# Retention, softplus and squared-ReLU layers on one core: another order for the head and the first half tile

## The chip, the cores and the metric
The kernel runs on one core of one Trainium2 chip. The metric is the device time of one execution in microseconds. The engines named here are TensorE (PE; its weight loads are listed as PEld), VectorE (DVE), ScalarE (ACT) and SyncE (SP), which issues most of the DMAs.

## The reference, cut to what matters
```python
# q, k, v: 4 batches, 8 heads, 576 tokens, 64 per head
scores = q @ k.T / 8                       # per batch and head
ret = scores * gamma[h] ** (i - j)         # only where i >= j, else 0
x = (ret @ v), heads side by side          # 2304 tokens x 512
h = x @ w_in;  g = max(h, 0) + log1p(exp(-|h|));  x = g @ w_out      # 512 -> 2048 -> 512
h = x @ w_in2; r = max(h, 0); g = r * r;          x = g @ w_out2     # 512 -> 2048 -> 512
```

## The kernel before
Retention runs in chunks of two times 64 tokens: a chunk is 1 MB of q, k (one DMA) and k, v (another). Each half of a chunk has a place s, 0 or 1, on the lower or the upper 64 partitions. For a chunk the kernel computes scores (small 64x64 matmuls), multiplies them with a mask, adds k times v to a running state (`states`), copies the state for the next half (`next_state`, two ScalarE copies) and forms the outputs from the masked scores and from the carried state (`outputs`). `scaled` multiplies the outputs with decay factors; the factors are spread over the partitions by small matmuls (`spread`) and products (`make_xw`).

The dense layers keep precision by splitting each operand into a high part (rounded to fp32r) and a low part, so each product is three matmuls. A weight arrives packed and takes five operations: two on ScalarE (L151, L152), one on VectorE (L156, "word operation"), a cast on ScalarE (L184) and a difference on VectorE (L185, the remainder). This is a generator, `split_w`, that is advanced by `pump_step` or `pump_to`; three staging buffers hold raw weights, and `pump_load` issues the next load when a buffer is free.

The first layer walks over five tiles of tokens (512, 384, 512, 512, 384) in steps. A step j does `g1` (L505: 12 matmuls into one bank), softplus (three ScalarE operations in `softplus_a`, three VectorE operations in `softplus_b`), `split_g` (cast and low part of g) of step j-1, and `g2` (L557: 12 matmuls into four accumulators) of step j-2. Between them it does one or two "visits" of retention for later tokens (`attend`, `visit`), and takes weights further. The first tile is done in two halves: steps 0 to 7 take its first eight blocks of the hidden layer, then tile 1 runs, then the other eight blocks of tile 0; its input x is kept in HBM (`x0d`) meanwhile.

Ahead of the steps is the head: the first four chunks (512 tokens), written out by hand under `manual_schedule`, which keeps the order of the source. Keep-warm matmuls of a zero tile (`keep_warm`, two records each) fill the start. The head shares four PSUM banks with the accumulators, converts three weights, and computes g1 of steps 0 and 1 for the first 256 tokens (`EARLY_G1`). Steps 0 to 7 are ordered by the framework's planner, the steps after them by the source.

Of the kernel before, what the change touches and what calls it, by code (L numbers as in the profile page):

```python
# [7 lines left out]
F32 = mybir.dt.float32  # L8
# [4 lines left out]
ALU = mybir.AluOpType  # L13
# [32 lines left out]
def kernel(  # L46
# [53 lines left out]
    ps_acc = ctx.enter_context(tc.tile_pool(name="ps_acc", bufs=4, space=PSUM))  # L100
# [3 lines left out]
    dram = ctx.enter_context(tc.tile_pool(name="dram", bufs=1, space=DRAM))  # L104

# [200 lines left out]

    x_raw = {}
# [126 lines left out]
    def scaled(c, s, po):  # L434
        m, _ = turn(c, s)
        t, off = tile_of((2 * c + s) * CN)
        if t == 0:
            x = ew.tile([P, 512], F32, tag="l", name="x")[:, :KD * CN]
            x = x.rearrange("p (a b) -> p a b", a=KD)
        else:  # L440
            if t not in x_raw:
                x_raw[t] = xs.tile([P, 512 // CN, KD, CN], F32, tag="xr", name="xr")
            x = x_raw[t][:, off // CN]
        xw = cst[:, C_XW + m * 256:C_XW + (m + 1) * 256].rearrange("p (a b) -> p a b", a=KD)
        nc.vector.tensor_tensor(out=x, in0=po, in1=xw, op=ALU.mult)
        if t == 0:
            h, l = (o[:, :, off:off + CN] for o in (x_hi(), x_lo()))
            nc.scalar.copy(h, x)
            return lambda: nc.vector.tensor_tensor(out=l, in0=x, in1=h, op=ALU.subtract)
# [37 lines left out]
    def in_heads(t):  # L487
        return t.rearrange("p (h c) -> p h c", c=CN)

    def g1(key, f, n, begin=0):
        if begin == 0:
            hps[key] = h_bank("ph")
        ph = hps[key]
        wh, wl = w_hi[0, "wi", f], w_lo[0, "wi", f]
        todo, rest = [], []
        for kk in range(KD):
            c = slice(kk * P, (kk + 1) * P)
            h, l = x_hi()[:, kk, begin:n], x_lo()[:, kk, begin:n]  # L500
            todo += [(wh[:, c], h), (wl[:, c], h)]
            rest.append((wh[:, c], l))
        todo += rest
        for j, (a, x) in enumerate(todo):
            nc.tensor.matmul(  # L505
                ph[:, begin:n], lhsT=a, rhs=x, start=(begin == j == 0),
                stop=(j == len(todo) - 1), skip_group_check=True,
            )
# [438 lines left out]
    EARLY_G1 = 2  # L947
    last = n_first
    with tc.manual_schedule():
        rows_in = xs.tile([P, SCN * KD * CN], F32, tag="xr", name="rows_in")  # L950
        for row in (0, CN):
# [3 lines left out]
        for half in (LO, HI):  # L955
            nc.scalar.dma_start(out=cst[half, :C_XW], in_=consts[CN:P, :C_XW])
# [24 lines left out]

        def acc_bank(name):
            return in_heads(ps_acc.tile([P, 512], F32, tag="at", name=name))[:, :HH]


        def early_s(c):
            pb = in_heads(ps_acc.tile([P, 512], F32, tag="at", name="pb"))
            for h in range(H):
                for half in (LO, HI):
                    nc.tensor.matmul(  # L990
                        pb[half, h, :], lhsT=chunk[c][half, 1, h, :], rhs=chunk[c][half, 0, h, :],
                        start=True, stop=True, skip_group_check=True,
                    )
            scale_v(c)
            nc.vector.tensor_tensor(
                out=chunk[c][:, 1], in0=pb,
                in1=cst[:, C_MASK:C_MASK + CN].unsqueeze(1).to_broadcast([P, H, CN]), op=ALU.mult,
            )

        pos = {}  # L1000

        def early_o(c):
            pos[c] = po = [acc_bank("po") for _ in range(2)]
            rounds(at_rounds((0, states(c, 0))), {})
            next_state(c, 0)
            rounds(
                at_rounds((0, outputs(c, 0, po[0]))),
                at_rounds((5, outputs(c, 1, po[1], False)), (13, states(c, 1))),
            )

        def early_x(c):
            for rest in [scaled(c, s, pos[c][s]) for s in range(2)]:
                rest()
            next_state(c, 1)

        early_s(0)
        early_o(0)
        early_x(0)
        early_s(1)
        make_xw(4, 5)  # L1020
        early_o(1)
        pump_step()
        early_x(1)
        pump_step()
        early_s(2)
        pump_step()
        early_o(2)
        early_s(3)
        early_x(2)
        g1(0, 0, P * 2)  # L1030
        pump_step()
        early_o(3)
        pump_step()
        g1(1, 1, P * 2)
        early_x(3)
        pump_step()
    tc.no_sync_barrier()
    for c in range(last):
        chunk.pop(c)
    first.__exit__(None, None, None)  # L1040
    late_wts.append(ctx.enter_context(tc.tile_pool(name="late", bufs=1, reuse_waits="tile")))
    tick[0] = 2 * last
# [3 lines left out]
    def visit(c, s):  # L1046
# [71 lines left out]
    def step(j, at_s, i):  # L1118
# [4 lines left out]
        g1(j, f, n, 2 * P if j < EARLY_G1 else 0)  # L1123
# [6 lines left out]
        for fn in low[:2]:  # L1130
            fn()
        softplus_b(j, n)
        for fn in low[2:]:
            fn()
        if j >= 1:
            split_g(j - 1, TILES[steps[j - 1][0]][1])
# [3 lines left out]
        if begun or n_split[0] < n_one:  # L1140
            pump_to(j)
        if done:
            done()
        if at_s == 0 and 0 <= i - (FH - 1 - KD) < KD:
            keep_x(i - (FH - 1 - KD))
# [22 lines left out]

    begun = []

    def pump_to(j):
        for made in begun:
            while not next(made):
                pass
            pump_load(n_used[0] + STAGES)
        begun.clear()
        goal = min(n_one, 4 + 2 * j if j < FH else 3 + 2 * FH + (j - FH))
        while n_split[0] < goal:
            count, make, args = items[n_split[0]]
            pump_load(n_used[0] + count)  # L1180
            made = make(*args)
            next(made)
            next(made)
            n_split[0] += 1
            n_used[0] += count
            begun.append(made)
# [7 lines left out]
    run(0, FH)  # L1194
    with tc.manual_schedule():
        run(FH, KF*last_b)
    run(KF*last_b, len(steps))
# [80 lines left out]
```

## Time and profile before
| what | value |
|---|---|
| median of 3 runs | 859.21 us (857.04 to 859.52) |
| profiled execution | 860.09 us, its span 858.3 us |
| busy share of the span | PE 98%, PEld 90%, DVE 79%, ACT 55% |
| clock granted to TensorE, mean | 0.981 |
| HBM read, written | 147.41 MB, 40.89 MB |

A granted clock of 1.00 is 2.4 GHz, 0.50 is 1.2 GHz. The shares are averages over stages with different limits, so they say little of the first 115 us, which the change touches. A busy PE is not a PE at its peak: records overlap, and their number and length both count.

### The profile page before, as it was taken

What the parts mean: (1) busy time and instruction counts of PE and PEld (TensorE: products, weight loads), DVE (VectorE), ACT (ScalarE), POOL (GpSimd) and SP (SyncE); (2) the same over time, 40 slices, a digit from 0 to 9 for tenths busy, and PEclk for the clock granted to TensorE, in tenths of its full rate; (3) what the DMA queues carried; (4) which work ended last, traced back from release to release, by engine and by line L of the source; (5) the groups of instructions that cost most, each with busy time, mean ns of one, the idle gap of its engine ahead of it and who ended that gap; (6) DMA issues with size and microseconds to landing.
All of it is one profiled execution on the core that took longest, in us unless ns stands there. A gap on an engine that the chain in (4) does not pass through costs nothing.

```text
span 858.3 us, 17849 instructions
## 1 busy us (share of the span) xinstructions
PE 839.0 (98%) x6688; PEld 768.6 (90%) x6688; DVE 680.6 (79%) x1266; ACT 473.9 (55%) x888; POOL 0.2 (0%) x4
## 2 busy tenths in 40 slices
PE   8899999999999999999999999999999999999998
PEld 7877799988788886888899999999999999999998
DVE  4579988878878878787899988888597986686964
ACT  4568888757656676676878621355321454111453
POOL 0000000000000000000000000000000000000000
PEclk9769999999999999999999999999999999999999
DMA  9337645545556664576676877888988888888885
GB/s 344 123 128 233 206 155 172 174 159 176 155 204 207 208 200 150 180 227 202 185 247 214 263 227 248 260 274 282 294 257 251 246 261 265 282 251 254 244 263 163
DMA packets 119512, 189.47 MB, mean 221 GB/s; under 512 B 10242, under 2 KB 64130, under 8 KB 119426
## 3 DMA queue, kind: packets, MB, share of 16 engines
q1 hardware_dynamic: 119264, 188.26, 68.9%
q8 instruction: 53, 0.87, 0.4%
q14 instruction: 31, 0.25, 0.1%
q10 hardware_dynamic: 164, 0.09, 0.0%
HBM read 147.41 MB, written 40.89 MB: 219 GB/s over the span
## 4 chain that ended last, share of the span: by engine, by line
PE 78%; DVE 9%; DMA 6%; ACT 5%; issue 2%; SPq 0%; DVEq 0%; ACTq 0%
PE acc L557 17%; PE ph L505 16%; PE py L758 9%; PE py L693 9%; PE pz L758 6%; PE px L693 6%; PE pz L693 6%; PE px L758 5%; PE po L417 2%; DVE l L529 1%; DVE e L526 1%; DMA wo_raw<-in_moe_w_out_dram 1%; PE st L394 1%; DMA ring<-in_qk_t_dram 1%; PE pb L369 1%
## 5 line engine op out<-in xcount | busy, mean ns | idle before, releaser
L505 PE MATMUL ph<-xh,wi 128*128 128x512 f32 (+2 forms) x656 | 149.0, 368 | 2.1 <-DVE ring L379 1.9
L505 PEld LDWEIGHTS ph<-xh,wi 128*128 128x128 f32 x656 | 119.6, 191 | 19.7 <-ACT ring L405 1.6
L557 PE MATMUL acc<-gl,woh 128*128 128x512 f32 (+1 forms) x320 | 120.1, 375 | 1.6 <-DVE gl L542 1.6
L557 PE MATMUL acc<-gh,woh 128*128 128x512 f32 (+1 forms) x320 | 121.0, 383 | 0.0
L557 PE MATMUL acc<-gh,wol 128*128 128x512 f32 (+1 forms) x320 | 119.4, 373 | 0.2 <-DVE wol L185 0.2
L526 DVE SCALAR_TENSOR_TENSOR e<-e 128x512 f32<-128x512 f32 (+1 forms) x80 | 51.0, 637 | 47.5 <-ACT l L521 46.5
L693 PE MATMUL py<-t,sring 128*128 128x384 f32 x432 | 88.2, 338 | 0.0
L505 PE MATMUL ph<-xl,wi 128*128 128x512 f32 (+2 forms) x328 | 81.8, 367 | 3.8 <-DVE xl L469 3.5
L519 ACT ACTIVATE e<-ph 128x512 f32<-128x512 f32 (+1 forms) x80 | 44.2, 553 | 65.9 <-PE ph L505 65.5
L693 PEld LDWEIGHTS py<-t,sring 128*128 128x128 f32 x432 | 75.3, 188 | 1.9 <-DVE uring L871 0.6
L505 PEld LDWEIGHTS ph<-xl,wi 128*128 128x128 f32 x328 | 59.9, 190 | 13.5 <-DVE xl L469 6.4
L557 PEld LDWEIGHTS acc<-gl,woh 128*128 128x128 f32 x320 | 60.7, 190 | 10.8 <-DVE gl L542 3.4
L557 PEld LDWEIGHTS acc<-gh,woh 128*128 128x128 f32 x320 | 60.8, 191 | 9.2 <-ACT gh L541 0.5
L733 ACT CAST gh<-g 128x384 fp32r<-128x384 f32 x84 | 43.0, 513 | 46.8 <-PE px L758 16.7
L557 PEld LDWEIGHTS acc<-gh,wol 128*128 128x128 f32 x320 | 60.8, 190 | 8.3 <-DVE wol L185 0.6
L733 ACT CAST gring<-g 128x384 fp32r<-128x384 f32 x84 | 43.2, 514 | 42.7 <-PE py L758 18.7
L719 DVE TENSOR_TENSOR gl<-g,gh 128x384 fp32r<-128x384 f32 x84 | 46.3, 556 | 19.2 <-ACT gh L733 18.9
L719 DVE TENSOR_TENSOR gring<-g,gring 128x384 fp32r<-128x384 f32 x84 | 46.7, 555 | 18.4 <-ACT gring L733 16.4
L867 ACT COPY uring<-px 128x384 f32<-128x384 f32 x24 | 11.5, 479 | 86.9 <-PE px L693 86.9
L693 PE MATMUL pz<-t,sring 128*128 128x384 f32 x288 | 58.7, 334 | 0.0
L693 PE MATMUL px<-t,sring 128*128 128x384 f32 x288 | 58.3, 336 | 0.0
L521 ACT ACTIVATE l<-e,cst 128x512 f32<-128x512 f32 (+1 forms) x80 | 54.5, 681 | 5.2 <-DMA x2d<-xo 1.8
(112 smaller groups left out, 1675.5 us busy)
## 6 DMA issues: line engine op xcount, KB each, us to landing
sring<-s2d SPq DMA_DIRECT2D x168, 256.0 KB, 3.2
sring<-o2d SPq DMA_DIRECT2D x168, 256.0 KB, 3.4
wi_raw<-in_moe_w_in_dram SPq DMA_DIRECT2D x32, 512.0 KB, 4.3
wo_raw<-in_moe_w_out_dram SPq DMA_DIRECT2D x32, 512.0 KB, 4.1
s2d<-ct SPq DMA_DIRECT2D x48, 256.0 KB, 2.6
o2d<-ct SPq DMA_DIRECT2D x48, 256.0 KB, 2.9
ring<-in_qk_t_dram SPq DMA_DIRECT2D x14, 512.0 KB, 4.9
ring<-in_kv_dram SPq DMA_DIRECT2D x14, 512.0 KB, 5.8
```

Source lines behind the costliest of these rows:

```text
L369: nc.tensor.matmul(pb[to, h, :], lhsT=kk[:, hh, :], rhs=qp[:, hh, :], start=True, stop=True, skip_group_check=True,)
L417: nc.tensor.matmul(po[(LO, HI)[hh % 2], hh // 2, :], lhsT=before[rows, hh, :] if carried else sv[:, hh, :], rhs=qp[:, hh, :] if carried el ...
L505: nc.tensor.matmul(ph[:, begin:n], lhsT=a, rhs=x, start=(begin == j == 0), stop=(j == len(todo) - 1), skip_group_check=True,)
L519: nc.scalar.activation(out=e, in_=ph[:, :n], func=AF.Abs)
L521: nc.scalar.activation(out=l, in_=e, func=AF.Ln, bias=below_one, scale=1.0 + 2.0**-23)
L526: nc.vector.scalar_tensor_tensor(out=e, in0=e, scalar=-2.0, in1=e, op0=ALU.add, op1=ALU.mult)
L557: nc.tensor.matmul(acc[j][:, :n], lhsT=a, rhs=x, start=(begin and m == 0), stop=(end and m == 2))
L693: nc.tensor.matmul(ps, lhsT=a, rhs=x, start=(first and m == 0), stop=(m == len(todo) - 1), skip_group_check=True,)
L719: nc.vector.tensor_tensor(out=out, in0=a, in1=b, op=ALU.subtract)
L733: nc.scalar.copy(h, src)
L758: nc.tensor.matmul(blocks[m], lhsT=a, rhs=x, start=(first and p == n == 0 and m in opens), stop=(p == NP - 1 and n == 2), skip_group_check ...
L867: nc.scalar.copy(s1, px)
```

## The change
The head gets its own four PSUM banks (`ps_head`, given back before the accumulators are made). It loads all four chunks before any weight. It handles both halves of a chunk in one VectorE operation of 512 elements where it used two of 256 (`early_x`, `early_low`), and interleaves the outputs of chunk c with the scores of chunk c+1, one half beside the other. It converts one weight in full and begins two more; the early halves of g1 go. The inputs x of the first tile are stored to `x0d` from the head by ScalarE's DMA queue; the four sums in `keep_x` go. Steps 0 to 7 run in source order, g1 of step 0 multiplies the high weights first, weights begun in a step are finished right after the next step's g1, and chunk 5 is loaded in step 0.
```diff
+    head = tc.tile_pool(name="ps_head", bufs=1, space=PSUM)
...
+    def pump_end():
+        for made in begun:
+            while not next(made):
+                pass
+            pump_load(n_used[0] + STAGES)
+        begun.clear()
...
-    def g1(key, f, n, begin=0):
+    def g1(key, f, n):
...
+        if key:
+            todo = [[w for two in zip(*todo[:2]) for w in two], todo[2]]
+        else:
+            todo = [todo[0], todo[2], todo[1]]
...
-    def keep_x(kk):
-        t = cvt.tile([P, 512], F32, tag="ct", name="x0")
-        nc.vector.tensor_tensor(
-            out=t, in0=x_hi()[:, kk].bitcast(F32), in1=x_lo()[:, kk].bitcast(F32), op=ALU.add
-        )
-        nc.sync.dma_start(out=x0d[:, kk], in_=t)
...
     def spread(dst, row, shape, eng):
-        rows = ps_acc.tile([P, 512], F32, tag="at", name="rows")[:, :shape[0] * shape[1]]
+        rows = ps_head.tile([P, 512], F32, tag="pb1", name="rows")[:, :shape[0] * shape[1]]
...
-        pump_load(1)
-        load_chunk(0)
-        load_chunk(1)
-        pump_load(2)
-        load_chunk(2)
-        load_chunk(3)
+        for c in range(last):
+            load_chunk(c)
         pump_load(3)
         load_chunk(last)
-        load_chunk(last + 1)
...
-        keep_warm(10)
+        keep_warm(18)
...
-        make_xw(1, 3)
-        keep_warm(10)
-        pump(1)
+        make_xw(1, 1)
+        keep_warm(3)
...
+        def early_o(c):
+            pos[c] = ps_head.tile([P, 2, 512], F32, tag="po", name="po")
+            po = [in_heads(pos[c][:, s])[:, :HH] for s in range(2)]
+            lower, upper = outputs(c, 0, po[0]), outputs(c, 1, po[1], False) + states(c, 1)
+            if c + 1 < last:
+                lower += early_scores(c + 1, LO)
+                upper += early_scores(c + 1, HI)
+            rounds(at_rounds((0, lower)), at_rounds((1, upper)))
+            next_state(c, 1)
+
+        def early_x(c):
...
+            nc.vector.tensor_tensor(
+                out=x, in0=pos.pop(c)[:, :, :256].rearrange("p s (a b) -> p s a b", a=KD),
+                in1=table[:, m:m + 2], op=ALU.mult,
             )
+            nc.scalar.copy(early_at(x_hi(), c), x)
+            kept_of.append(kept)
+
+        def early_keep(c):
+            nc.scalar.dma_start(out=x0d[:, :, c * P:(c + 1) * P], in_=kept_of[c])
...
+        rounds(at_rounds((0, early_scores(0, LO))), at_rounds((0, early_scores(0, HI))))
+        scale_v(0)
+        early_mask(0)
+        keep_warm(4)
+        make_xw(2, 2)
+        early_states(0)
         early_o(0)
+        scale_v(1)
         early_x(0)
+        early_mask(1)
+        early_states(1)
+        early_low(0)
         make_xw(4, 5)
...
+        early_mask(3)
+        early_states(3)
+        early_low(2)
         pump_step()
         early_o(3)
+        keep_warm(8)
+        early_x(3)
+        early_keep(2)
         pump_step()
-        g1(1, 1, P * 2)
-        early_x(3)
+        early_low(3)
         pump_step()
+        pump_begin(3)
+        early_keep(3)
...
-            pb = in_heads(h_bank("pb", False))[:, :HH]
+            if c == last:
+                pb = in_heads(ps_at.tile([P, 512], F32, tag="at", name="pb"))[:, :HH]
+            else:
+                pb = in_heads(h_bank("pb", False))[:, :HH]
...
-        g1(j, f, n, 2 * P if j < EARLY_G1 else 0)
+        g1(j, f, n)
+        if at_s == 0 and i < FH - 1:
+            pump_end()
...
-        if begun or n_split[0] < n_one:
-            pump_to(j)
+        pump_end()
+        pump_to(j)
+        if j == 0:
+            load_chunk(last + 1)
...
-    run(0, FH)
+    run(0, 0)
     with tc.manual_schedule():
-        run(FH, KF*last_b)
+        run(0, KF * last_b)
```

## Rows read from the trace of the kernel before
**Rows 1.** Busy time by stage: stretch, length, busy us, granted clock, DMA share, GB/s.
```profile
8.00:20.40 12.40, 9.73 (x245) 9.22 (x245) 8.37 (x15) 5.77 (x13) 0.00 (x0) 0.99 1.03 393
20.40:33.50 13.10, 12.62 (x202) 12.00 (x200) 6.40 (x13) 5.18 (x13) 0.00 (x0) 0.50 0.43 160
...
44.50:57.60 13.10, 13.10 (x129) 9.76 (x126) 10.07 (x21) 7.59 (x14) 0.00 (x0) 0.50 0.17 58
...
70.00:95.70 25.70, 23.85 (x279) 18.71 (x278) 23.75 (x44) 22.90 (x42) 0.00 (x0) 1.00 0.77 253
95.70:113.80 18.10, 17.76 (x123) 15.62 (x121) 15.10 (x28) 14.60 (x27) 0.00 (x0) 1.00 0.58 184
113.80:160.00 46.20, 46.16 (x387) 45.40 (x388) 39.78 (x74) 40.62 (x77) 0.00 (x0) 1.00 0.45 142
```
**Rows 2.** Timeline of PE, gaps before the clock fell: start, length, work, idle before.
```profile
19.07 0.27 PE L417 MATMUL po<-ch,ring 64*64 64x64 f32 x2 [1.31 <-issue]
...
44.20 0.79 PE L394 MATMUL st<-ring 64*64 64x64 f32 x9 [3.17 <-ACT ring L405]
```
**Rows 3.** Timeline of PE in the head.
```profile
1.04 4.64 PE L912 MATMUL cold<-warm 128*128 128x128 f32 x20 [1.04 <-DVE warm L906]
5.61 1.28 PE L929 MATMUL rows<-rows_in,ones 1*64 1x256 f32 x8
6.82 4.00 PE L912 MATMUL cold<-warm 128*128 128x128 f32 x20
10.75 1.15 PE L990 MATMUL pb<-ch 64*64 64x64 f32 x32
...
25.38 1.23 PE L417 MATMUL po<-ch 64*64 64x64 f32 x32
...
34.27 0.69 PE L417 MATMUL po<-ch 64*64 64x64 f32 x32
34.80 0.63 PE L417 MATMUL po<-ch,ring 64*64 64x64 f32 x16
```
**Rows 4.** Timeline of PE, steps 7, 8 and 11.
```profile
90.48 2.08 PE L505 MATMUL ph<-xh,wi 128*128 128x512 f32 x8 [1.21 <-DVE ring L379]
...
93.30 0.39 PE L557 MATMUL acc<-gh,woh 128*128 128x512 f32 x1
...
96.02 1.57 PE L505 MATMUL ph<-xh,wi 128*128 128x384 f32 x8
...
112.11 0.86 PE L505 MATMUL ph<-xl,wi 128*128 128x384 f32 x4
```
**Rows 5.** Timeline of ACT, softplus of step 7 and weight operations.
```profile
95.70 0.60 ACT L519 ACTIVATE e<-ph 128x512 f32<-128x512 f32 x1
...
97.00 0.73 ACT L521 ACTIVATE l<-e,cst 128x512 f32<-128x512 f32 x1
...
101.19 0.62 ACT L184 CAST wi<-ct 128x512 fp32r<-128x512 f32 x1
...
102.23 0.67 ACT L151 ACTIVATE wi_raw<-wi_raw 128x512 f32<-128x512 f32 x1
102.80 0.75 ACT L152 ACTIVATE wi_raw<-wi_raw,cst 128x512 uint32<-128x512 uint16 x1
```
**Rows 6.** Timeline of DVE, steps 3 and 7 and the drain.
```profile
64.49 0.68 DVE L532 SCALAR_TENSOR_TENSOR e<-ph,l 128x512 f32<-128x512 f32 x1
65.09 0.41 DVE L445 TENSOR_TENSOR xr<-po,cst 128x256 f32<-128x256 f32 x1
...
96.13 1.96 DVE L469 TENSOR_TENSOR xl<-xr,xh 128x384 fp32r<-128x384 f32 x4
...
108.56 1.28 DVE L567 COPY xo<-acc 128x512 f32<-128x512 f32 x2
```
**Rows 7.** DMA issues up to 110 us: KB each, median us from issue to landing.
```profile
wi_raw<-in_moe_w_in_dram SPq DMA_DIRECT2D x12, 512.0 KB, 4.2
...
ring<-in_qk_t_dram SPq DMA_DIRECT2D x5, 512.0 KB, 7.2
```

More of the change, by code (lines that the diff above doesn't have):

```diff
@@ L104 @@
     dram = ctx.enter_context(tc.tile_pool(name="dram", bufs=1, space=DRAM))
+    head = tc.tile_pool(name="ps_head", bufs=1, space=PSUM)
+    ps_head = head.__enter__()
     cst = const.tile([P, C_ALL], F32, name="cst")
@@ L304, in pump, with pump_begin @@
                     break
+    begun = []
+    def pump_end():
[4 more added lines that the diff above has]
+        begun.clear()
+    def pump_begin(upto):
+        while n_split[0] < min(n_one, upto):
+            count, make, args = items[n_split[0]]
+            pump_load(n_used[0] + count)
+            made = make(*args)
+            next(made)
+            next(made)
+            n_split[0] += 1
+            n_used[0] += count
+            begun.append(made)
     x_raw = {}
@@ L436, in scaled @@
         t, off = tile_of((2 * c + s) * CN)
[L437 to L443, printed above, removed]
-        xw = cst[:, C_XW + m * 256:C_XW + (m + 1) * 256].rearrange("p (a b) -> p a b", a=KD)
[L445 to L449, printed above, removed]
+        if t not in x_raw:
+            x_raw[t] = xs.tile([P, 512 // CN, KD, CN], F32, tag="xr", name="xr")
+        xw = cst[:, C_XW + m * 256:C_XW + (m + 1) * 256].rearrange("p (a b) -> p a b", a=KD)
+        nc.vector.tensor_tensor(out=x_raw[t][:, off // CN], in0=po, in1=xw, op=ALU.mult)
     tick = [0]
@@ L488, in in_heads @@
         return t.rearrange("p (h c) -> p h c", c=CN)
-    def g1(key, f, n, begin=0):
-        if begin == 0:
-            hps[key] = h_bank("ph")
-        ph = hps[key]
+    def g1(key, f, n):
+        ph = hps[key] = h_bank("ph")
         wh, wl = w_hi[0, "wi", f], w_lo[0, "wi", f]
-        todo, rest = [], []
+        todo = [[], [], []]
         for kk in range(KD):
             c = slice(kk * P, (kk + 1) * P)
[L500 to L503, printed above, removed]
+            h, l = x_hi()[:, kk, :n], x_lo()[:, kk, :n]
+            for part, a, x in zip(todo, (wh, wl, wh), (h, h, l)):
+                part.append((a[:, c], x))
+        if key:
+            todo = [[w for two in zip(*todo[:2]) for w in two], todo[2]]
+        else:
+            todo = [todo[0], todo[2], todo[1]]
+        todo = sum(todo, [])
         for j, (a, x) in enumerate(todo):
             nc.tensor.matmul(
-                ph[:, begin:n], lhsT=a, rhs=x, start=(begin == j == 0),
-                stop=(j == len(todo) - 1), skip_group_check=True,
+                ph[:, :n], lhsT=a, rhs=x, start=(j == 0), stop=(j == len(todo) - 1)
             )
@@ L945, in make_xw @@
         )
-    EARLY_G1 = 2
     last = n_first
@@ L950 @@
         rows_in = xs.tile([P, SCN * KD * CN], F32, tag="xr", name="rows_in")
+        for half in (LO, HI):
+            nc.scalar.dma_start(out=cst[half, :C_XW], in_=consts[CN:P, :C_XW])
         for row in (0, CN):
@@ L977 @@
         spread(times, row[:, 1:, :, 0], (SCN - 1, KD), nc.scalar.copy)
-        make_xw(1, 3)
-        keep_warm(10)
-        pump(1)
[L982 to L994, printed above, removed]
+        make_xw(1, 1)
@@ new lines, with early_scores @@
+        keep_warm(3)
+        pbs, pos, xs_of, kept_of = {}, {}, {}, []
+        def early_scores(c, half):
+            if c not in pbs:
+                pbs[c] = in_heads(ps_head.tile([P, 512], F32, tag=f"pb{c % 2}", name="pb"))
+            return [
+                lambda h=h: nc.tensor.matmul(
+                    pbs[c][half, h, :], lhsT=chunk[c][half, 1, h, :], rhs=chunk[c][half, 0, h, :],
+                    start=True, stop=True, skip_group_check=True,
+                ) for h in range(H)
+            ]
@@ L995, in early_s, with early_mask, early_states @@
+        def early_mask(c):
             nc.vector.tensor_tensor(
-                out=chunk[c][:, 1], in0=pb,
+                out=chunk[c][:, 1], in0=pbs.pop(c),
                 in1=cst[:, C_MASK:C_MASK + CN].unsqueeze(1).to_broadcast([P, H, CN]), op=ALU.mult,
             )
-        pos = {}
-        def early_o(c):
-            pos[c] = po = [acc_bank("po") for _ in range(2)]
+        def early_states(c):
             rounds(at_rounds((0, states(c, 0))), {})
             next_state(c, 0)
-            rounds(
-                at_rounds((0, outputs(c, 0, po[0]))),
-                at_rounds((5, outputs(c, 1, po[1], False)), (13, states(c, 1))),
-            )
@@ L1011, in early_x @@
[L1011 to L1016, printed above, removed]
+        def early_o(c):
[7 more added lines that the diff above has]
+            next_state(c, 1)
@@ new lines, in early_x @@
+        def early_x(c):
+            m = 2 * c
+            x = ew.tile([P, 512], F32, tag="e", name="x", bufs=3)
+            kept = x.rearrange("p (a n) -> p a n", a=KD)
+            x = xs_of[c] = x.rearrange("p (a s b) -> p s a b", s=2, a=KD)
+            table = cst[:, C_XW:].rearrange("p (m a b) -> p m a b", a=KD, b=CN)
+            nc.vector.tensor_tensor(
+                out=x, in0=pos.pop(c)[:, :, :256].rearrange("p s (a b) -> p s a b", a=KD),
+                in1=table[:, m:m + 2], op=ALU.mult,
+            )
+            nc.scalar.copy(early_at(x_hi(), c), x)
+            kept_of.append(kept)
@@ new lines, in early_keep, with early_at, early_low @@
+        def early_keep(c):
+            nc.scalar.dma_start(out=x0d[:, :, c * P:(c + 1) * P], in_=kept_of[c])
+        def early_at(t, c):
+            return t[:, :, c * P:(c + 1) * P].rearrange("p a (s b) -> p s a b", s=2)
+        def early_low(c):
+            nc.vector.tensor_tensor(
+                out=early_at(x_lo(), c), in0=xs_of.pop(c), in1=early_at(x_hi(), c),
+                op=ALU.subtract,
+            )
+        rounds(at_rounds((0, early_scores(0, LO))), at_rounds((0, early_scores(0, HI))))
@@ L1017 @@
+        scale_v(0)
[3 more added lines that the diff above has]
+        early_states(0)
         early_o(0)
+        scale_v(1)
         early_x(0)
-        early_s(1)
+        early_mask(1)
+        early_states(1)
+        early_low(0)
         make_xw(4, 5)
         early_o(1)
-        pump_step()
+        scale_v(2)
         early_x(1)
-        pump_step()
-        early_s(2)
-        pump_step()
+        early_keep(0)
+        early_mask(2)
+        early_states(2)
@@ L1039 @@
         chunk.pop(c)
+    head.__exit__(None, None, None)
     first.__exit__(None, None, None)
     late_wts.append(ctx.enter_context(tc.tile_pool(name="late", bufs=1, reuse_waits="tile")))
+    ps_acc = ctx.enter_context(tc.tile_pool(name="ps_acc", bufs=4, space=PSUM))
     tick[0] = 2 * last
@@ L1129, in step @@
         later = attend(at_s, i)
-        for fn in low[:2]:
+        if False and j:
+            split_g(j - 1, TILES[steps[j - 1][0]][1])
+        for fn in low:
             fn()
         softplus_b(j, n)
-        for fn in low[2:]:
-            fn()
-        if j >= 1:
+        if j and not (False):
             split_g(j - 1, TILES[steps[j - 1][0]][1])
@@ L1166, in step @@
                     build_t(m)
-    begun = []
     def pump_to(j):
[L1172 to L1186, printed above, removed]
+        pump_begin(4 + 2*j if j<FH else 3+2*FH+(j-FH))
     order = [(at_s, i) for at_s, (_, f0, f1) in enumerate(segments) for i in range(f1 - f0)]
@@ L1192, in run @@
             step(j, *order[j])
-    run(0, FH)
+    run(0, 0)
     with tc.manual_schedule():
-        run(FH, KF*last_b)
-    run(KF*last_b, len(steps))
+        run(0, KF * last_b)
+    run(KF * last_b, len(steps))
     j = len(steps)
```

10 lines of the change are left out of this document (3 added, 7 removed).

## The prediction, on record before the changed kernel was run
> **What bounds the kernel now.** I read the busy time by stage first, then the timelines of TensorE, ScalarE and VectorE over the first 115 us, and last the DMA issues. In the stages the reader sees two stretches of about 13 us each in which the granted clock is 0.50, the lower level of 1.2 GHz: 20.4 to 33.5 (the head, all small 64x64 matmuls) and 44.5 to 57.6 (steps 0 to 2) [rows 1]. Before the first fall TensorE ran small matmuls with gaps, the longest 1.31 us; before the second it sat idle for 3.17 us, waiting for ScalarE's state copies [rows 2]. From 70 to 95.7 VectorE is busy 23.75 of 25.70 us and TensorE 23.85. From 95.7 on TensorE is last: 17.76 of 18.10, then 46.16 of 46.20 [rows 1]. So I read the change at one mark, the end of g1 of step 11, 112.11 + 0.86 = 112.97 [rows 4]. Behind it the program is the same and TensorE sets the pace: what is gained or lost by then is gained or lost in the whole.
>
> I call S(j) the start of step j's first softplus operation on ScalarE (before: S(7) = 95.70 [rows 5]).
>
> **The change, part by part.**
> *Start.* Ten keep-warm pairs end at 1.04 + 4.64, ten more cost 4.00 [rows 3], so 0.40 each; eighteen end at 8.9. The spread took 1.28 with two banks; now both rows share one bank, so the second waits for the copy of the first. That wait is not in the trace. From below it is 0; from above a whole second spread, 1.28. I take 0.7, since only one copy lies between: 10.9. Three pairs: 12.1, and there the scores of chunk 0 begin, 1.35 later than the 10.75 of before [rows 3]. They take 1.15 (1.0 to the next start), four pairs 1.6 cover the mask: 14.75.
>
> *Chunks.* Matmuls of one half alone go 16 in 0.63, of both halves in two banks 32 in 0.69 [rows 3]; less the tail of about 0.15 that all share that is 33 and 17 ns. The new order runs outputs, states and next scores of the two halves beside each other. The longer, upper half sets it: 32 + 16 + 16 records at 33 ns, 2.1, with its lag and the same-bank rounds 2.4. Before each goes states(c,0), 0.55, and a wait for the state copies of about 0.3; the mask (0.7) runs beside these. About 3.35 a chunk. Chunk 0 goes 14.75 to 17.75, chunk 1 to 21.1, chunk 2 to 24.5, chunk 3, without next scores, to 27.2, where its outputs ended at 34.80 + 0.63 = 35.4 before [rows 3]. VectorE needs four operations of 0.60 to 0.69 a chunk, so 2.6, beside it. The wider operation on two banks is not in the trace; bounds are 0.60, a plain 128x512 operation, and twice that; I take the first, the same element count [rows 6]. The second bound would add under 1 us in all, since it waits beside the scores.
>
> *First matmul step.* Eight pairs, 3.2, end at 30.4. Beside them VectorE scales (27.6), ScalarE copies the state and casts x (28.6) and casts the first weight (about 29.6). Then g1(0) at the full clock, 93.30 - 90.48 = 2.8 [rows 4]: 33.2. The early halves of g1 in the head go; they were the same matmuls, so nothing is lost there. ScalarE has two weights begun (four operations, 2.5 [rows 5]), two DMA issues of 0.4 and two casts: S(0) at 33.5.
>
> *Step 0.* It holds two visits of chunk 4 that share a bank: scores, mask (behind the two weight remainders on VectorE), scale of v, then states and scores, then mask again, and only then softplus' VectorE part. With VectorE's starts 0.60 apart (65.09 - 64.49 [rows 6]) that part ends at 39.8, the weight's word operation at 40.4, its cast on ScalarE at 41.0; with full durations instead it is 42.4. I take S(1) = 42.0. TensorE idles nearly 3 us between the two visits, as it did before the second fall; if the clock falls there, g1(1) costs up to 2.8 more, of which softplus of step 1 sees about 0.5, as it waits for ScalarE anyhow.
>
> *Steps 1 to 6.* Source order closes a loop between two engines: softplus on ScalarE (95.70 to 97.73, 2.0 [rows 5]), three VectorE operations of 0.68, each waiting for the one before (2.0), the low part of g 0.60, scaled outputs 0.41, scale of v 0.60 in every second step, two word operations 1.2 [rows 6], a cast of 0.52 [rows 5], some 0.3 of handing over: 7.0 or 7.6. ScalarE alone needs 6.6, VectorE 6.3, TensorE 2.8 for g1, 96.02 - 93.30 = 2.7 for g2 [rows 4] and about 1.15 for a visit (32 small matmuls [rows 3]), 6.7 together, so the loop is last. S(6) = 42.0 + 7.6 + 7.0 + 7.6 + 7.0 + 7.6 = 78.8. The four sums of x (0.60 each) are gone from this stretch; their stores are the four ScalarE issues in the head, 1.6, half of it beside TensorE.
>
> *Loads.* Chunks first: 4.3 MB at 393 GB/s [rows 1] land by 13, three weights by 17, chunk 4 by 20, all before use (15 for chunk 1, 24 and 33 for the others). Chunk 5 is now issued at about 33 behind three weights; a chunk's q and k took 7.2 us from issue to landing [rows 7], so 40, and its visit is due at about 40: up to 1 us of TensorE, beside S(1). The second weight of each step is issued when its buffer comes free, about 1.2 before S(j), and wanted 4.4 after it; 4.2 to landing [rows 7] leaves about 1.
>
> *Into tile 1.* From S(6): casts of the new x on VectorE at 6.9, its four low parts 1.96 [rows 6], 8.8; softplus 2.0 and the low part of g, 11.4; g2(6) 2.7, g1(9) 2.1 (8 of its 12 take 1.57 [rows 4]): 16.2; g2(7), waiting for its low part until 16.4, 19.1; g1(10) 21.2; the four banks are drained (the VectorE pair 1.28 [rows 6]) by 23.2, g2(8) ends at 24.1, g1(11) at 26.2.
>
> *Sum.* The mark comes at 78.8 + 26.2 = 105.0 instead of 112.97: 8.0 gained. The profiled execution took 860.09 (span 858.3 and 1.8 around it), so 852.1; it lies 0.9 above the median of the runs, so against the median I forecast **851.5**.
>
> **The clock in the head** is the widest open point. What rows show: it fell at 20.4, some 9.6 us after the last full-array matmul, in a stretch that was busy 9.73 of 12.40 us, and then small matmuls at 12.62 of 13.10 did not raise it [rows 1]; full-array g1 did. After the change the small matmuls run from 14.75 to 27.2, 12.5 us, with fuller overlap and gaps under 0.8 us. The Trainium skill ("TensorE: Matmul & The Clock Gate", section "Why this matters for your kernels") ties throughput drops to idle gaps between bursts of matmuls and asks for continuous work. By that rule the head stays at 2.4 GHz and the sum holds; the trace agrees at the second fall (3.17 us idle), less at the first (1.31 us at most). If instead small matmuls alone let it fall, and as long after the last full-array one as before, it falls at 14.75 + 9.6, about 24.
>
> **Rivals.**
> *A, the head goes to 1.2 GHz at 20 to 22.* For it: 32 matmuls took 1.23 at the lower level against 0.69 [rows 3], and small matmuls alone held neither level before. Against it: gaps are shorter than where it fell. Price: chunks 2 and 3 cost some 5.3 more, and the eight pairs about 1.7 more; g1(0) comes at 37.5, S(1) is 5.5 to 6 later. Gain 2 to 2.5, 857.
> *B, in-order waits (slower).* With source order ScalarE's queue stops at the first operation on a weight that has not landed, and softplus of the next step is behind it; before, the order let other work pass. The mechanism sits at the second weight of each step and decides from a landing more than 5.6 us after issue. If weights take the 7.2 of the chunks they share the engines with [rows 7], each of steps 1 to 6 costs 1.6 to 2 more, 10 in all: gain -2, 861 to 862, and more where a chunk load goes ahead of them. Against it: the weights' 4.2, and DMA busy only 0.77 from 70 to 95.7 [rows 1].
> *C, the loop is shorter than I hold,* TensorE's 6.7 sets the step and S(1) is 41: S(6) at 74.5, gain 12, 847.
> *D, the new order isn't a new order:* the engines' order came out much as before and only the chunk part differs; then steps 1 to 7 keep their length and 1 to 2 us remain, 858.
>
> **How the numbers follow.** Forecast 0.58 (848.5 to 855), A 0.19, B 0.11, C 0.08, D 0.04. A change under 0.3% (2.6 us) can't be told from none here, so "same" is 856.6 to 861.8. Faster: forecast and C whole and half of A, 0.75; same: half of A, D and a little of B, 0.15; slower: most of B, 0.10. The range is 846.5 to 859, which leaves out B and the tail of C.
>
> **What would show it.** Right: granted clock 1.00 up to 30 us; last chunk's outputs at about 27, g1(0) at about 30; S(0) to S(7) 7 to 7.6 apart with VectorE's word operations as releaser of ScalarE's casts; g1(11) ending near 105. Wrong: a clock of 0.50 before 25 (A); ScalarE idle with weight DMAs as releaser in steps 1 to 6 (B); TensorE without gaps from step 1 (C). The forecast fails if the mark is later than 110.

## The result, and the profile after

| | median | executions |
|---|---|---|
| before | 859.28 us | 857.04 to 863.58 (6) |
| after | 848.75 us | 847.87 to 851.23 (6) |

Ratio 0.988, 95% interval 0.9852 to 0.9908: faster by 10.5 us, forecast 7.7. The profiled execution after took 847.87, its span 846.1 (before 858.3), its mean granted clock 0.996 (before 0.981).

Busy time by stage after, the columns and stretches of [rows 1]:

```profile
8.00:20.40 12.40, 10.36 (x272) 8.89 (x272) 7.45 (x11) 3.29 (x9) 0.00 (x0) 0.95 1.03 379
20.40:33.50 13.10, 12.80 (x285) 11.52 (x281) 7.99 (x13) 10.06 (x21) 0.00 (x0) 0.91 0.45 123
44.50:57.60 13.10, 12.06 (x153) 9.47 (x153) 11.99 (x22) 11.87 (x21) 0.00 (x0) 1.00 0.63 204
70.00:95.70 25.70, 22.22 (x183) 18.30 (x184) 23.12 (x42) 23.75 (x44) 0.00 (x0) 1.00 0.61 203
95.70:113.80 18.10, 17.76 (x153) 16.34 (x152) 14.75 (x28) 14.96 (x30) 0.00 (x0) 1.00 0.55 173
113.80:160.00 46.20, 46.20 (x365) 45.49 (x364) 38.26 (x71) 40.02 (x75) 0.00 (x0) 1.00 0.53 160
```

Where [rows 1] show 0.99, 0.50 and 0.50 the reader sees 0.95, 0.91 and 1.00. TensorE after, the lines that answer to [rows 2 to 4]:

```profile
1.04 6.45 PE L918 MATMUL cold<-warm 128*128 128x128 f32 x36 [1.04 <-DVE warm L912]
...
10.75 1.15 PE L988 MATMUL pb<-ch 64*64 64x64 f32 x32
...
18.45 0.27 PE L439 MATMUL po<-ch,ring 64*64 64x64 f32 x2 [1.43 <-issue]
...
28.13 2.05 PE L918 MATMUL cold<-warm 128*128 128x128 f32 x16
30.47 1.19 PE L519 MATMUL ph<-xh,wi 128*128 128x512 f32 x4 [0.29 <-ACT wi L185]
...
35.99 0.86 PE L391 MATMUL pb<-ring 64*64 64x64 f32 x16 [1.89 <-DVE ring L401]
...
105.30 0.86 PE L519 MATMUL ph<-xl,wi 128*128 128x384 f32 x4
```

The scores of chunk 0 start at 10.75, as before. The chunks are over at 28.13, some 7 us earlier than before, g1(0) (g1 of step 0) starts at 30.47, and the mark, the end of g1(11), is 105.30 + 0.86 = 106.16, so 6.8 us earlier [rows 4]. The gap of 1.43 at 18.45 is one that the forecast did not hold; the clock was at 0.50 behind it, from 19.27 to 22.68, and again behind the gap at 35.99, from 36.34 to 39.75.

ScalarE after, three of the starts S(j) and a cast that waits, the view of [rows 5]:

```profile
63.75 0.60 ACT L532 ACTIVATE e<-ph 128x512 f32<-128x512 f32 x1
...
71.06 0.60 ACT L532 ACTIVATE e<-ph 128x512 f32<-128x512 f32 x1
...
78.00 0.62 ACT L185 CAST wi<-ct 128x512 fp32r<-128x512 f32 x1 [1.31 <-DVE ct L157]
...
79.25 0.60 ACT L532 ACTIVATE e<-ph 128x512 f32<-128x512 f32 x1
```

The casts wait for VectorE's word operation ("<-DVE ct L157"): the loop between the two engines that the forecast drew. Steps 1 to 5 took 7.6, 7.3, 7.6, 7.3 and 8.2.

How far a kernel is ahead of the kernel before at S(j), from such lines of five profiled executions, one of each kernel. "Low alone", "without low" and "planner" are experiments below:

| | before | after | after is ahead by | low alone | without low | planner |
|---|---|---|---|---|---|---|
| S(0) | 39.49 | 34.27 | 5.2 | 0.9 | 4.3 | 4.0 |
| S(7) | 95.70 | 85.94 | 9.8 | 2.1 | 7.0 | 8.3 |
| S(9), tile 1 | 103.49 | 96.86 | 6.6 | 1.7 | 0.3 | 8.4 |
| S(31) | 216.71 | 210.15 | 6.6 | 1.7 | 0.3 | 8.3 |
| S(32), tile 2 | 224.42 | 215.82 | 8.6 | 3.7 | 0.3 | 10.4 |
| S(48), tile 3 | 328.56 | 319.16 | 9.4 | 4.8 | 0.3 | 11.4 |
| S(79), end of tile 4 | 490.01 | 477.44 | 12.6 | 7.3 | 0.3 | 13.9 |

The lead of 6.6 at S(9) stays to S(31) and then grows by 6.0, at the starts of tiles 2, 3 and 4 and within tile 4. The head can't do that. One line of the change does, `for fn in low[:2]` made `for fn in low`: where a new tile begins all four low parts of the next tile's x now go ahead of the VectorE part of softplus, where two went ahead and two behind. The cut diff ahead of the prediction leaves it out. What it does at the start of tile 2, before; first VectorE, then TensorE, then the stages:

```profile
219.29 1.29 DVE L469 TENSOR_TENSOR xl<-xr,xh 128x512 fp32r<-128x512 f32 x2
...
222.55 1.28 DVE L469 TENSOR_TENSOR xl<-xr,xh 128x512 fp32r<-128x512 f32 x2
```

```profile
223.28 1.10 PE L505 MATMUL ph<-xl,wi 128*128 128x512 f32 x2 [1.77 <-DVE xl L469]
...
325.13 1.10 PE L505 MATMUL ph<-xl,wi 128*128 128x512 f32 x2 [1.68 <-DVE xl L469]
```

```profile
224.00:228.00 4.00, 4.00 (x71) 3.16 (x72) 3.76 (x7) 3.51 (x7) 0.00 (x0) 0.63 0.45 145
```

The second pair of low parts starts 3.3 us after the first, and TensorE stands 1.77 us for it; then the clock is 0.63 in the mean of 224 to 228. At the start of tile 3 the same wait is 1.68 (second line of TensorE), and there the clock stays at 1.00. After, at the start of tile 2, in the same views (the stage 8 us earlier, as this kernel is 8.6 ahead there):

```profile
212.73 2.49 DVE L482 TENSOR_TENSOR xl<-xr,xh 128x512 fp32r<-128x512 f32 x4
215.14 0.69 DVE L539 SCALAR_TENSOR_TENSOR e<-e 128x512 f32<-128x512 f32 x1
```

```profile
214.34 1.45 PE L519 MATMUL ph<-xl,wi 128*128 128x512 f32 x4
```

```profile
216.00:220.00 4.00, 3.18 (x69) 2.64 (x62) 3.90 (x7) 3.92 (x8) 0.00 (x0) 1.00 0.16 52
```

All four go in one block, TensorE's four matmuls on them follow without a listed wait (1.45 in all, 1.07 where nothing holds them), and the clock stays at 1.00.

### The profile page after: what moved, and what is told of

It reads as the page before. It is cut to its first block, busy times and chain, and to the rows that moved or that the text cites. A ratio compares the mean times of both kernels' runs of the same rounds, so it can differ in the third digit from the quotient of the medians.

```text
span 846.1 us, 17836 instructions
## 1 busy us (share of the span) xinstructions
PE 826.1 (98%) x6690; PEld 759.2 (90%) x6690; DVE 678.9 (80%) x1255; ACT 474.2 (56%) x884; POOL 0.2 (0%) x4
## 4 chain that ended last, share of the span: by engine, by line
PE 82%; DVE 8%; ACT 5%; DMA 2%; issue 2%; ACTq 0%; SPq 0%; DVEq 0%
PE acc L570 19%; PE ph L519 18%; PE py L764 9%; PE py L699 9%; PE pz L764 6%; PE px L699 6%; PE pz L699 6%; PE px L764 5%; PE po L439 2%; DVE xl L482 1%; DVE l L542 1%; PE st L416 1%; DVE e L539 1%; DMA ring<-in_qk_t_dram 1%; DVE gl L555 1%
## 5 line engine op out<-in xcount | busy, mean ns | idle before, releaser
L519 PE MATMUL ph<-xh,wi 128*128 128x512 f32 (+1 forms) x640 | 147.0, 371 | 2.4 <-ACT l L534 1.1
L519 PEld LDWEIGHTS ph<-xh,wi 128*128 128x128 f32 x640 | 117.6, 189 | 19.2 <-issue 1.4
L519 PE MATMUL ph<-xl,wi 128*128 128x512 f32 (+1 forms) x320 | 79.0, 368 | 0.1
```

The source lines that it names most:

```text
L519: nc.tensor.matmul(ph[:, :n], lhsT=a, rhs=x, start=(j == 0), stop=(j == len(todo) - 1))
```

## The experiments

**Without the low order (head and source order remain).** In `step`:
```diff
-        for fn in low:
+        for fn in low[:2]:
             fn()
         softplus_b(j, n)
+        for fn in low[2:]:
+            fn()
```


> The changed kernel, but where a new tile of x is split into high and low parts two of the four low parts again come behind softplus on VectorE, as before. Theory 'three places': the gain of 12.2 us in the span is 6.6 from the head and the first half tile (step 11's softplus starts 6.6 earlier and stays so), some 2.5 from the order of the four low parts at tile boundaries and some 3 from the last tile, whose order the planner chooses differently behind it. It then expects step 11 at 107.5 as after, but no further gain: step 79's softplus 6.6 before that of the kernel before, the granted clock low again near 215 to 225, and 854 us. Rival 'all from the head' (what the prediction held): the low parts are hidden, 848.5 to 849.5 us.

Measured: 855.44 (850.17 to 858.85), ratio 0.9966 (0.9943 to 0.9989). So without this line only 3.2 of the 10.5 us are left. Its profiled execution took 858.81, 3.4 above the median, and shows the worst case: a lead of 7.0 at S(7) is gone at S(9), where I expected 6.6 to stay. VectorE, TensorE and stages of that execution:

```profile
89.10 1.02 DVE L482 TENSOR_TENSOR xl<-xr,xh 128x384 fp32r<-128x384 f32 x2
...
92.86 1.02 DVE L482 TENSOR_TENSOR xl<-xr,xh 128x384 fp32r<-128x384 f32 x2
```

```profile
93.46 0.91 PE L519 MATMUL ph<-xl,wi 128*128 128x384 f32 x2 [1.55 <-DVE xl L482]
...
95.74 0.80 PE L570 MATMUL acc<-gh,wol 128*128 128x512 f32 x1 [0.68 <-DVE wol L186]
```

```profile
96.00:100.00 4.00, 4.00 (x10) 3.13 (x11) 3.93 (x8) 3.12 (x6) 0.00 (x0) 0.50 0.63 198
```

TensorE waits 1.55 for the late low parts and 0.68 for a weight queued behind them; from 94.88 to 101.71 the clock is 0.50. The kernel before does not have this: there the planner had put all four in one block at the entry into tile 1, at 96.13 [rows 6], whatever the source said. So at this one boundary the line makes good what source order would cost, and the 3.2 is not the worth of the head and the order by themselves.

**The low order alone, on the kernel before.** The opposite edit: `for fn in low[:2]` made `for fn in low`, the loop over `low[2:]` left out, nothing else.

> The kernel before, with nothing changed but the order of the four low parts (all ahead of softplus on VectorE). 'Three places': steps up to 31 as before, from step 32 on 2.0 to 2.8 earlier, in the last tile 5.5, time 853.5 to 854. 'All from the head': 859, no step moves by more than 0.5.

Measured: 853.63 (853.28 to 854.70), ratio 0.9936 (0.9913 to 0.9959). One line is worth 5.0 us, half of the whole change. In the table its lead of 1.7 at S(9) is already there at S(7), ahead of the first low part, so it is the head's own variation; 5.6 come later, as 'three places' had it.

**Source order alone, on the kernel before.**
```diff
-    run(0, FH)
     with tc.manual_schedule():
-        run(FH, KF*last_b)
+        run(0, KF*last_b)
```
(and chunk 4's scores in a bank of their own)

> The kernel before with its own head, but steps 0 to 7 in source order (and the scores of chunk 4 in the bank that the change uses, without which the order can't run). Theory 'the loop of source order is the gain': steps 1 to 6 are 7.3 to 8 apart instead of 9.2 in the mean, step 7's softplus at 91 to 93 instead of 95.7, time 855 to 857. Rival 'the head is the gain': step 7 at 95 to 97, 859.

Measured: 871.85, ratio 1.0141 (1.0107 to 1.0176): 13 us slower, where I expected no loss. In the main this is rival B, on the old head. Up to S(8) ScalarE has four such waits; they add to 8.9, and S(8) comes 9.0 later than before. Two of them:

```profile
57.13 0.67 ACT L151 ACTIVATE wo_raw<-wo_raw 128x512 f32<-128x512 f32 x1 [2.97 <-DMA wo_raw<-in_moe_w_out_dram]
...
97.99 0.67 ACT L151 ACTIVATE wo_raw<-wo_raw 128x512 f32<-128x512 f32 x1 [2.98 <-DMA wo_raw<-in_moe_w_out_dram]
```

The first operation on a weight that has not landed holds ScalarE's queue for up to 3.0 us. Another 3.0 are lost from S(8) to S(9), and they are not B: source order also takes the low parts apart at the entry into tile 1, as in the run without the low order, and TensorE waits for the second pair:

```profile
106.39 1.16 PE L505 MATMUL ph<-xl,wi 128*128 128x384 f32 x2 [3.07 <-DVE xl L469]
```

**The planner's order, on the changed kernel.** Steps 0 to 7 back to the planner: `run(0, FH)`, then `run(FH, KF * last_b)` in source order.

> The changed kernel with its new head, but steps 0 to 7 ordered by the planner again. Theory 'the loop of source order is the gain': planner's order brings back bubbles, step 7's softplus at 89 to 91 instead of 85.9, time 852 to 854. Rival 'the head is the gain': step 7 within 1 of 85.9, time 848 to 850.

Measured: 847.59 (846.47 to 848.25), ratio 0.9865 (0.9842 to 0.9888). The time is that of the rival, 'the head is the gain', though S(7) came 1.5 later than after, at 87.43, and not within 1. The source order thus gives nothing here; the difference to 848.75 is within the intervals. Where it costs: TensorE at the entry into tile 1, first after, then with the planner:

```profile
89.15 0.85 PE L519 MATMUL ph<-xl,wi 128*128 128x384 f32 x4
...
90.95 0.50 PE L570 MATMUL acc<-gl,woh 128*128 128x512 f32 x1 [0.70 <-DVE gl L555]
92.15 0.50 PE L570 MATMUL acc<-gh,wol 128*128 128x512 f32 x1 [0.70 <-DVE wol L186]
...
94.56 1.57 PE L519 MATMUL ph<-xh,wi 128*128 128x384 f32 x8
```

```profile
89.27 0.94 PE L519 MATMUL ph<-xl,wi 128*128 128x384 f32 x4
...
92.79 1.57 PE L519 MATMUL ph<-xh,wi 128*128 128x384 f32 x8
```

From the low half of g1(8) to g1(9) 5.41 us go by in source order, with waits for VectorE (0.70 twice), and 3.52 with the planner.

**Fewer keep-warm matmuls.** `keep_warm(18)` made `keep_warm(10)`; `keep_warm(4)` and `keep_warm(8)` left out.

> The changed kernel with fewer keep-warm matmuls: the first group of 18 pairs cut to 10, the groups of 4 and of 8 in the middle and at the end of the head left out (they compute nothing that is used). Theory A (the head's real matmuls hold TensorE's clock, the keep-warm groups cost only their own time): scores(0) starts at 10.75 as now, since it waits for its load; the first words of softplus S(0) come 0 to 1 us before 34.27, the windows of the head keep granted clocks within 0.1 of .95 and .91, the time is 847.5 to 849. Theory B (the groups hold the clock): the clock is 0.5 in part of 8 to 33 us more than the 3.4 us it has now, S(0) comes 1 to 3 us after 34.27, and the time is 850 to 853.

Measured: 852.97 (851.26 to 857.04), ratio 0.9943 (0.9919 to 0.9967), S(0) at 37.58: theory B by its time, and S(0) came 3.3 later, a little more than it had. The trace tells most of it another way. The clock was 0.50 from 8.82 to 12.23, behind the shorter first group, where the changed kernel had 1.00; but until 17 the chunks are up to 0.6 us ahead of the changed kernel. Then TensorE stands 2.93 us where it stood 1.43, and the clock is low behind it (TensorE, then the stage):

```profile
20.24 0.59 PE L439 MATMUL po<-ch 64*64 64x64 f32 x11 [2.93 <-issue]
```

```profile
20.00:28.00 8.00, 7.76 (x202) 7.71 (x202) 3.28 (x5) 2.13 (x6) 0.00 (x0) 0.50 0.20 65
```

Whether the missing matmuls made the standstill longer is open.

**Halves apart.** `early_x` and `early_low` as two VectorE operations each, one per half of the chunk.

> The changed kernel with the one VectorE operation for two chunk halves taken apart again: the product with the table, and the low part, are two operations each, eight more in all in the head. Theory A (VectorE has idle time between the chunks, so this part of the change is worth nothing): S(0) at 34.27 within 0.5, time 848 to 849.5. Theory B (VectorE paces the head): eight more starts of 0.1 to 0.25 us each, 0.8 to 2 us at S(0), time 849.5 to 851.

Measured: 847.55 (846.64 to 848.65), S(0) at 35.32. One operation for two halves is worth nothing in time: theory A (its S(0), 1.05 later, missed the bound by half a microsecond, its time lies 0.45 below A's range, and at S(6) 0.1 of the delay was left).

**The low order of before at the last boundary only.** As in the first experiment, where the next tile is tile 4.

> The changed kernel with the low parts of x two ahead of and two behind the softplus words at the last boundary alone (tile 3 into tile 4), as in the kernel before; at the other boundaries all four ahead. Theory A (the gain behind the head comes from two places: the first boundary, and the last boundary with the planner's order of tile 4 behind it): S(8) to S(60) as in the changed kernel (6.6 to 9.4 us ahead of the kernel before), S(79) 9 to 10 ahead in place of 12.6, time 851 to 852.5. Theory B (the order at the last boundary costs nothing, the rest of tile 4 follows from the start of it): S(79) as in the changed kernel, time 848.5 to 849.5.

Measured: 850.11 (847.84 to 851.15). S(63) is as after (0.1 earlier), S(79) is 2.8 later: theory A in the trace. The time is 1.4 above 848.75 and below the 851 that I gave, and the executions overlap.

**Chunk 4 loaded later.** `load_chunk(last)` from ScalarE's queue behind `early_x(0)`.

> The changed kernel with the load of chunk 4 (1 MB, not needed before step 0) issued from ScalarE's queue behind the first high part of x, at about 17 to 18 us, in place of 11.5 to 12.7 us from SyncE's. TensorE stands 1.43 us at 17 to 18.5 us with nothing that it waits for, while the DMA share is 1.08 to 1.12. Theory A (what it waits for there is its instructions, which come by the same saturated DMA engines): that gap is under 0.4 us, the granted clock does not fall to 0.5 at 19.2, S(0) comes 1 to 2.5 us before 34.27, time 846 to 848. Theory B (the gap has another cause): a gap of 1 us or more stays within 2 us of that place, S(0) within 0.5 of 34.27, time 848 to 849.5.

Measured: 848.26 (848.10 to 848.46), a gap of 1.45 before 18.18: theory B by the gap and the time; its S(0) is missed, 35.31, behind a second gap of 1.45 before 22.97. But the DMA share stayed at 1.04 to 1.11 from 14 to 20, as the weights were still under way, so it did not test theory A.

**Word operations later in the loop.** `pump_end()` behind `softplus_b` in steps 1 to 7, and their g1 in the order high-high, high-low, low-high.

> The changed kernel with two orders changed in steps 0 to 7: the second group of word operations (high part of the weight, low part of the weight) comes behind the softplus words in place of ahead of them, and the matmuls of the first product go high-high, high-low, low-high. The steps 1 to 6 take 7.0 to 8.2 us each (S(1) 41.21 to S(6) 79.25), of which the matmuls fill about 5; the traces name ScalarE's cast waiting for VectorE's words (0.74 to 1.31) and TensorE for VectorE's masked scores. Theory A (the word operations between the softplus words hold the loop): S(2) to S(6) spaced 6.4 to 7.1, S(7) 2 to 4 us before 85.94, time 845 to 847. Theory B (the sum of the loop's operations is the same in any order, or the load of the weights paces it): S(7) within 0.7 us of 85.94, time 848 to 849.5. Theory C (words that come later delay the product of the next step): S(7) 1 to 4 us later, time 850 to 853.

Measured: 849.10 (846.58 to 850.41). The loop did get shorter, S(5) came 1.6 earlier, and it was all given back by S(7), 86.08 against 85.94. One of the waits that took its place, on TensorE:

```profile
71.64 0.27 PE L391 MATMUL pb<-ring 64*64 64x64 f32 x2 [1.48 <-DMA ring<-in_qk_t_dram]
```

A chunk's load is issued when its ring buffer comes free; a faster loop runs into its landing. Theory B, by the load.

**Step 7 alone by the planner.** `run(0, FH - 1)` in source order, `run(FH - 1, FH)` by the planner.

> The changed kernel with step 7 alone ordered by the planner, steps 0 to 6 in source order as changed. In the run with all eight steps by the planner S(7) came at 87.43, later than 85.94 in source order, but S(9) at 95.09 in place of 96.86. Theory A (the gain of the planner lies in step 7, where it may put the start of tile 1 ahead): S(7) at 86.0, S(9) at 93.6 to 95, time 845.5 to 847.5. Theory B (the gain needs the planner's order of the steps before): S(9) at 96.5 to 97, time 848 to 849.5.

Measured: 848.14 (847.53 to 848.88), S(9) at 97.06: theory B by its numbers, but the trace is not clean. S(1) came 1.7 late in it, with the clock at 0.50 until 42.96 where the changed kernel has 39.75. From S(6) to S(9) it took 16.7, the changed kernel 17.6 and the planner's eight steps 14.7. So step 7 alone gave 0.9 of the 2.9; that the rest needs the earlier steps is argued, not shown.

**A quiet stretch of DMA.** The three weight loads and chunk 4 made to wait for chunk 0's x:
```diff
+        mark.append(xs_of[0][0:1, 0, 0, 0:1])
         pump_load(3)
         load_chunk(last)
...
+        for m in mark:
+            nc.vector.tensor_copy(t.bitcast(F32)[0:1, 0:1, 0], m)
```


> The changed kernel with the first three loads of weights (1.5 MB) and that of chunk 4 (1 MB) held back: each waits for one more copy of a single element that VectorE makes from chunk 0's x (five in all, at about 15.7), so that the DMA engines, at a share of 1.01 to 1.15 from 13 to 20 us in the changed kernel, stand idle from about 13 to 17. TensorE stands there without a wait that the profile shows (1.43 us before 18.45, 0.64 to 2.93 in the other runs), 1 to 3 us behind the one packet of the instruction queue in that stretch. Theory A (its instructions come late because they share the DMA engines with these loads): that gap falls below 0.4, no clock of 0.5 follows it, S(0) at 32.3 to 33.8 unless the weights are then late; time 847 to 849, as runs with S(0) one us earlier had no more than 0.1 left at S(6). Theory B (the gap is the fetch itself, whatever else moves): a gap of 0.6 us or more within 16 to 20 us; S(0) 34.9 to 36.

Measured: 852.24 (848.41 to 852.61), ratio 0.992 (0.9896 to 0.9944). Stages and TensorE:

```profile
14.00:16.00 2.00, 2.00 (x73) 1.81 (x74) 0.50 (x1) 0.73 (x2) 0.00 (x0) 0.97 0.00 0
16.00:18.00 2.00, 2.00 (x60) 1.94 (x61) 1.31 (x7) 1.14 (x3) 0.00 (x0) 1.00 0.00 0
20.00:22.00 2.00, 1.93 (x48) 1.72 (x42) 2.00 (x4) 1.04 (x3) 0.00 (x0) 1.00 1.09 362
24.00:26.00 2.00, 2.00 (x66) 1.88 (x59) 1.24 (x2) 1.25 (x3) 0.00 (x0) 1.00 1.01 377
28.00:30.00 2.00, 0.71 (x27) 0.71 (x30) 0.00 (x0) 0.24 (x1) 0.00 (x0) 0.50 0.11 30
```

```profile
22.85 0.27 PE L445 MATMUL po<-ch,ring 64*64 64x64 f32 x2 [0.81 <-issue]
...
29.29 0.37 PE L445 MATMUL po<-ch,ring 64*64 64x64 f32 x2 [3.10 <-issue]
```

With the DMA engines idle (0.00) TensorE runs without a standstill. They are busy again from 18.5 on, and then it stands 0.81 and 3.10 us; the clock falls to 0.50 and S(0) comes at 38.10. In the changed kernel, with the loads under way, the same view has:

```profile
16.00:18.00 2.00, 1.02 (x25) 0.83 (x23) 1.66 (x3) 1.43 (x4) 0.00 (x0) 1.00 1.08 353
20.00:22.00 2.00, 2.00 (x45) 2.00 (x43) 0.55 (x1) 1.21 (x3) 0.00 (x0) 0.50 0.25 92
```

So theory A held at the place that I had named, and its times were wrong: the standstill moved to where the loads went. The last one outlasted them: from 27.5 on the DMA share was 0.2, and TensorE stood until 29.29.

**Planner and shorter loop together.** The edits of the fourth run and of the one on the loop.

> All eight steps of the first half tile ordered by the planner, on the new head and with the low parts ahead (847.6 in the earlier run), and the two orders of the run on the loop: the second group of word operations behind the softplus words, the matmuls high-high, high-low, low-high. Theory A (the two gains add: the loop was 1.6 us ahead at S(5) there, before a chunk's load in the ring held it, and the planner spares 1.8 to 3 us at the start of tile 1): S(9) at 93.5 to 95.1, time 845.5 to 847. Theory B (the load of the ring, or the planner's own order, leaves nothing of the first): S(9) 95 to 96, time 847 to 848.5.

Measured: 849.01 (847.60 to 850.14), S(9) at 97.82. Both theories missed S(9), by 1.8 us and more; S(0) was already 1.8 later than after. No version is shown to beat the changed kernel: 847.55 and 847.59 lie within its interval.

## Why the prediction was right, and where it was not

The time lay in the range, but two errors met in it, and that they went opposite ways was luck. (The sum's own 8.0, set against the median of 859.21, gives 851.2, not the 851.5 that I forecast.)

*The failed step* is "Behind it the program is the same and TensorE sets the pace: what is gained or lost by then is gained or lost in the whole." The program behind the mark is not the same: the low parts moved at later boundaries too, and TensorE's pace there held waits of 1.77 and 1.68 us and, behind one of them, a low clock. Profile against profile 12.2 us were gained, 6.8 at the mark and 5.4 behind it, for which I had 0. In medians the line alone is worth 5.0 on the kernel before and 6.7 on the changed one, where it also mends the entry into tile 1.

*The sum to the mark,* 8.0, was too large: 6.8 in the trace. In medians what is not the line gives 3.2 (without it) to 4.9 (from 853.63 to 848.75). Source order gave none of it: with the planner's order the new head and the line together gave 11.0 (858.62 to 847.59), so 6.0 are left to the head if the line's 5.0 simply add. The new head by itself, without the line and with the planner's order, was not run, and which of its parts gain is open but for the one operation for two halves (nothing) and the keep-warm matmuls (848.75 against 852.97). By terms:
- *Start:* forecast 12.1, measured 10.75. Eighteen pairs took 6.45, 0.36 each and not 0.40, and the scores follow right behind the three pairs, as this term had it.
- *Chunks:* forecast 27.2, measured 28.13 despite the earlier start. In between lie the standstill of 1.43 and 3.4 us at a clock of 0.50. The time of a chunk was right: 3.3 from states(0) at 12.92 to states(1) at 16.23, where neither interfered, forecast 3.35, though (0.63 - 0.15)/16 is 30 ns and not the 33 of the working; the stop was not among its terms, although the kernel before had one of 1.31 with the same releaser [rows 2].
- *First matmul step and step 0:* g1(0) forecast 30.4, measured 30.47; S(0) 33.5 and 34.27; S(1) 42.0 and 41.21. The low clock at 36 to 40 that I allowed for came, beside ScalarE's wait, and moved S(1) little: with halves apart it did not come, and from S(0) to S(1) 6.6 went by in place of 6.9.
- *Steps 1 to 6:* forecast 7.6 and 7.0, measured 7.6 and 7.3, with the releaser named. S(6) 78.8 and 79.25. The last step's 8.2 has a wait of 1.31 for the word operation.
- *Into tile 1:* forecast 26.2, measured 106.16 - 79.25 = 26.9. All four low parts went as one block, as this part assumed from [rows 6]. What I did not see is that only the planner had made them one block before: in source order it takes the new line, and without it S(9) came 6.3 later.

*Rivals.* A (clock) is the head's real risk: 1.00 up to 30 us, my sign for being right, did not come. The clock fell, for a shorter time than A had, and where it fell for longer the time was 852 to 853. My ground for A, that small matmuls alone let it fall, was wrong. With the planner's order, where small matmuls fill 20 to 28:

```profile
20.00:28.00 8.00, 7.29 (x300) 6.77 (x292) 6.03 (x9) 4.98 (x12) 0.00 (x0) 1.00 0.30 91
```

They ran at 1.00; TensorE's longest standstills there and just ahead were 0.57 and 0.51. In the chunks of the other heads a low clock came behind longer ones, of 1.3 to 3.1 us (once of 0.93, 2 us behind one of 1.28). The rule of the Trainium skill that I cited ("TensorE: Matmul & The Clock Gate", "Why this matters for your kernels"), which ties it to idle gaps, agrees with that in kind. In size it does not: it warns of longer gaps than those of 1.3 to 1.9 us behind which the clock fell in most of these heads, and the measurement decides. Nor are gaps the whole: a gap of 1.45 at 18.18 (chunk 4 later) left the clock at 1.00 until 22, and from 11 to 14 the planner's head had 0.50 behind the spread where the changed kernel, busy 3.11 of 4.00 us from 7 to 11 and the planner's head 3.43, had 1.00. Why, stays open.

B did not happen in the changed kernel, where ScalarE waits for no load from 34 to 100, and cost some 9 of the 13 us on the old head, so it belonged to the case. What spares the changed kernel from it (weights finished earlier, or loads in another order) no run took apart. C and D are out: the loop is 7.3 to 7.6 long, and S(1) to S(7) are all new.

## What to carry to other kernels

Go through every hunk of the diff and ask at which steps it runs; a line in a helper that runs at each tile boundary can be worth as much as a rewritten head. When an engine that is nearly full is waited for at a boundary, put what the waiting engine needs in one block ahead of the rest. A planner may already do so where the source does not, so look at the trace of such a boundary before giving it another order. A shorter loop helps only as far as the loads that its buffers release keep up, so work out the next wait before the edit.

## What the runs showed of the hardware

In the head of each of these profiles TensorE stood still for 0.4 to 3.1 us among small matmuls, with nothing that the profile shows to wait for (the state copies that its next matmul reads had ended 0.7 us before in the changed kernel, 2.4 us before the longest). These standstills came behind the same number of its recorded instructions, matmuls and weight loads together, in every kernel: 443, 697 to 699 or 953, so some 255 apart. The old head and the new one have this alike, and so does the run with fewer keep-warm matmuls, where the next matmul reads no state copy. Each ended 2.2 to 2.7 us after one packet of 16 KB on the DMA queue for instructions had started, however long it was: the packet started at 15.89 and TensorE went on at 18.45 in the changed kernel, 17.59 and 20.24 with fewer keep-warm matmuls, 26.87 and 29.29 in the run with the quiet stretch. Where the packet came earlier there was no standstill: with the loads held back the first started at 13.06, the DMA share fell to 0.00, and TensorE went past the 443rd instruction at 18.23 without a stop. That points to TensorE waiting for its own instructions. Which instructions a packet carries the profile doesn't show, so it is not proved. That other loads hold the packet back is less sure still: the share was mostly 0.5 to 1.1 during the standstills, and one run alone, with the loads held back, had the packet early (behind 169 recorded instructions; 342 to 443 in the others).
